# One run of 64x64 matmuls per pair of head pairs: scores of the second token tile in four array quadrants, and a new order of all work

## The chip, the cores and the metric

One Trainium2 chip, of which the program uses one core. The time is that of the device, in microseconds (us), for one execution of the whole program; the time before is 775.9 us, the median of 3 runs (774.52 to 779.68).

## The reference

Attention within chunks of 64 tokens, then a feed-forward part whose nonlinearity is h*cos(h):

```
q, k, v: (8, 8, 576, 64)      # batch, heads, tokens, head dimension
s    = (q_c @ k_c^T) / 8                    # per head and chunk: 64x64
p    = exp(s - max(s)) / (sum + 1e-9)       # over the last axis
x    = p @ v_c, heads side by side          # 4608 tokens x 512
h    = x @ w_in                             # 512 -> 2048
out  = (h * cos(h)) @ w_out                 # 2048 -> 512
```

All is fp32 at the outside. The wide products are made of three fp32r products each (high times high, high times low, low times high).

## The kernel before, in words

The 4608 tokens are 9 tiles of 512. A tile has 8 chunks of 64 tokens and 8 heads, taken as 4 head pairs of 128 partitions (two heads of 64 each). For each tile there are the scores, the softmax, the transposed weights, the weighted values, and from those `x`, which is split in a high and a low part for the feed-forward products.

**Small matmuls.** Scores and weighted values are 64x64 matmuls, which use one quadrant of the 128x128 array each: a quadrant is a half of the rows (where the input partitions stand) and a half of the columns (where the output partitions stand). fp32 matmuls show as two passes each in the profile, so a program's x32 is x64 there. `scores_early` (L525) is for tiles 0 and 1: head 0 of the pair uses the upper left quadrant, head 1 the lower right one, 16 matmuls per head pair into one PSUM bank. `scores_of_pair` (L558) is for tiles 2 to 8: the head chooses the rows, the parity of the chunk the columns, so all four quadrants are used in turn, and two head pairs share two banks (`scores`, L572: 32 matmuls). `weighted_of_pair` (L692) uses four quadrants too.

**Stages.** Tiles 0 and 1 are made plainly: `hidden` (L752, 12 matmuls into a bank `h` for each of 16 blocks of 128 hidden units), `activated` (L764: ScalarE, VectorE, ScalarE, VectorE, then the split of `g`) and `project` (L786). Block s needs the bank of block s-2, which is free when `g<-h,g` (L777) has read it. Tiles 2 to 8 go through a scheme with 7 products for 8 (`two_pairs` L1579, `block_pair` L1848): products A11, S3, S2, A12, S1, A22, S4, in that order, with copies of a bank by ScalarE (L1018) and sums by VectorE (L1021) between them. The attention of a later tile is worked in between these products: `scores_now` (L2285) and `weighted_now` (L2347).

**Order.** The program first writes a list of pieces of work, each with its engine, what it must come after, and an estimated length; then it emits them sorted by the numbers of the table `RANK` (L92), and on the other engine that could do it where the table `ELSEWHERE` (L287) says so (`in_order`, L311). Each engine runs its list strictly as it stands. In `scores_now` and `weighted_now` the 32 matmuls are two pieces of 16, between which the table may put other matmuls; in `early` (L1195), for tile 1, each head pair's scores are a piece.

Of the kernel before, what the change touches and what calls it, by code (L numbers as in the profile page):

```python
# [317 lines left out]
def attention_then_cos_ffn(ctx: ExitStack, tc, qT, kT, v, w_in, w_out, out, wide):  # L318
# [239 lines left out]
    def scores_of_pair(t, g, j, banks):  # L558

        qt, kt = queries.pop((t, 2 * g + j))  # L560
        for c in range(NCH):
# [3 lines left out]
            for h in range(2):  # L565
                hs = slice(h * CH, (h + 1) * CH)
                matmul(
                    banks[h][ps, o : o + CH], qt[hs, cs], kt[hs, cs], start=(o == 0), stop=True,
                    skip_group_check=True,
                )  # L570

    def scores(t, g, banks):  # L572

        for j in range(0 if t > FAST else 2):
            scores_of_pair(t, g, j, banks)
# [2005 lines left out]
```

## Time and profile before

| | |
|---|---|
| median of 3 runs | 775.9 us |
| profiled execution | 775.4 us, span of its records 773.5 us |
| mean granted TensorE clock | 0.998 |
| TensorE (PE) busy | 756.7 us, 98% |
| VectorE (DVE) busy | 675.3 us, 87% |
| ScalarE (ACT) busy | 530.0 us, 69% |
| GpSimd (POOL) busy | 351.8 us, 45% |

PE counts matmuls; a matmul's record runs on after the next has begun, so a distance between two starts tells what one costs, and the duration does not. A row of the timeline merges neighbours of one kind: start, time, what, count, and in brackets the idle time before it with what ended it.

### The profile page before, as it was taken

Reading aid. Unit: us, or ns where it says so; the run is one execution under the profiler, and the core shown is the slowest. Engines: PE = TensorE matmul, PEld = TensorE weight load, DVE = VectorE, ACT = ScalarE, POOL = GpSimd, SP = SyncE. Lnnn points to the kernel's source line nnn. Section 1 sums busy time; section 2 is a strip of 40 time slices with the busy share of each in tenths; the row PEclk is TensorE's granted clock in tenths of the full one; section 3 lists DMA queues with packets and bytes.
Section 4 is the critical chain, followed back from the end, with each engine's and each line's share of the span. In section 5 each row is a group of like instructions: output and inputs, shape, how many; then the busy total and the mean of one; then the engine's idle time right before and its main releaser. Section 6 shows DMA issues by size and latency. Waiting matters only on the chain.

```text
span 773.5 us, 18066 instructions
## 1 busy us (share of the span) xinstructions
PE 756.7 (98%) x6680; PEld 683.9 (88%) x6680; DVE 675.3 (87%) x1129; ACT 530.0 (69%) x1067; POOL 351.8 (45%) x335
## 2 busy tenths in 40 slices
PE   7899999999999999999999999999999999999998
PEld 6688888888999898888889998888899989989997
DVE  4898779889899998989999979989999889878985
ACT  5898787455786466878786659879786556567632
POOL 2443252654589325745732145547501236464143
PEclk9999999999999999999999999999999999999999
DMA  9990631289989857898899956899899567999982
GB/s 345 410 417 28 210 134 57 93 283 342 361 290 332 293 185 247 294 311 258 308 330 380 362 182 240 263 324 326 288 364 342 183 189 251 307 315 337 347 279 99
DMA packets 127001, 210.92 MB, mean 273 GB/s; under 512 B 11713, under 2 KB 67009, under 8 KB 126913
## 3 DMA queue, kind: packets, MB, share of 16 engines
q1 hardware_dynamic: 126336, 208.71, 77.8%
q8 instruction: 53, 0.87, 0.4%
q10 hardware_dynamic: 576, 1.05, 0.4%
q14 instruction: 36, 0.29, 0.1%
HBM read 148.90 MB, written 60.82 MB: 271 GB/s over the span
## 4 chain that ended last, share of the span: by engine, by line
PE 74%; DVE 9%; DMA 8%; ACT 4%; issue 3%; POOL 1%; SPq 0%; ACTq 0%; DVEq 0%; POOLq 0%
PE acc L352 31%; PE h L352 27%; PE a L352 15%; DMA sums<-w_in 4%; DVE w_in L373 2%; DMA w_in<-diffs 2%; DVE w_in L1027 1%; DMA sums<-g 1%; DMA w_in<-in_w_in_dram 1%; DMA x<-sums 1%; ACT w_in L1024 1%; DVE g_lo L373 1%; DVE w_in L686 1%; POOL w_in L373 1%; DVE g L373 1%
## 5 line engine op out<-in xcount | busy, mean ns | idle before, releaser
L352 PE MATMUL h<-x,w_in 128*128 128x512 f32 (+1 forms) x960 | 225.0, 365 | 0.8 <-DVE g L777 0.4
L352 PEld LDWEIGHTS h<-x,w_in 128*128 128x128 f32 x960 | 169.0, 190 | 22.3 <-DVE g L777 1.1
L352 PE MATMUL acc<-w_out,g_hi 128*128 128x512 f32 (+1 forms) x720 | 172.7, 330 | 0.0
L352 PEld LDWEIGHTS acc<-w_out,g_hi 128*128 128x128 f32 x720 | 123.8, 190 | 12.4
L352 PE MATMUL acc<-w_out,g_lo 128*128 128x512 f32 (+1 forms) x360 | 117.4, 326 | 0.0
L352 PE MATMUL h<-w_in,w_in 128*128 128x512 f32 (+1 forms) x384 | 98.7, 355 | 2.0 <-ACT h L1018 1.1
L373 POOL TENSOR_TENSOR w_in<-w_in,w_in 128x512 f32<-128x512 f32 (+2 forms) x41 | 48.8, 1195 | 60.1 <-ACT w_in L1031 27.2
L352 PEld LDWEIGHTS h<-w_in,w_in 128*128 128x128 f32 x384 | 65.4, 190 | 11.8 <-ACT h L1018 3.2
L352 PEld LDWEIGHTS acc<-w_out,g_lo 128*128 128x128 f32 x360 | 68.6, 191 | 4.7
L369 ACT CAST g_hi<-w_in 128x512 fp32r<-128x512 f32 x71 | 44.0, 623 | 34.2 <-PE acc L352 14.9
L1031 ACT ACTIVATE w_in<-w_in 128x512 f32<-128x512 f32 x96 | 57.8, 628 | 12.3 <-DVE w_in L1027 12.0
L373 POOL TENSOR_TENSOR g_lo<-w_in,g_hi 128x512 fp32r<-128x512 f32 x32 | 42.3, 1321 | 38.0 <-ACT g_hi L369 19.2
L373 DVE TENSOR_TENSOR g_lo<-w_in,g_hi 128x512 fp32r<-128x512 f32 x62 | 45.5, 737 | 4.2 <-ACT g_hi L369 3.5
L369 ACT CAST g_hi<-x 128x512 fp32r<-128x512 f32 x52 | 32.2, 622 | 22.4 <-PE acc L352 12.0
L373 POOL TENSOR_TENSOR g_lo<-x,g_hi 128x512 fp32r<-128x512 f32 x9 | 12.3, 1372 | 74.9 <-ACT g_hi L369 74.9
L1024 ACT ACTIVATE w_in<-w_in 128x512 int32<-128x512 f32 x56 | 34.1, 627 | 15.8 <-DVE w_in L1021 11.9
L373 POOL TENSOR_TENSOR g_lo<-g,g_hi 128x512 fp32r<-128x512 f32 x20 | 26.8, 1342 | 38.6 <-ACT g_hi L369 25.7
L352 PE MATMUL a<-w_in,w_in 128*128 128x512 f32 (+1 forms) x204 | 43.1, 350 | 1.0 <-ACT w_in L369 0.7
L352 PE MATMUL a<-x,w_in 128*128 128x512 f32 (+1 forms) x192 | 41.2, 353 | 0.0
L352 PE MATMUL acc<-w_in,g_hi 128*128 128x256 f32 x240 | 41.1, 275 | 0.0
L373 DVE TENSOR_TENSOR g_lo<-x,g_hi 128x512 fp32r<-128x512 f32 x47 | 36.5, 788 | 5.1 <-ACT g_hi L369 4.8
L1027 DVE SCALAR_TENSOR_TENSOR w_in<-w_in,w_in 128x512 f32<-128x512 int32 x56 | 37.7, 696 | 2.4 <-ACT w_in L1024 1.7
(316 smaller groups left out, 1957.4 us busy)
## 6 DMA issues: line engine op xcount, KB each, us to landing
w_in<-combo SPq DMA_DIRECT2D x84, 512.0 KB, 5.4
w_in<-sums SPq DMA_DIRECT2D x64, 256.0 KB, 5.2
combo<-w_in SPq DMA_DIRECT2D x56, 256.0 KB, 4.3
w_in<-combo SPq DMA_DIRECT2D x56, 256.0 KB, 5.5
x<-sums SPq DMA_DIRECT2D x48, 256.0 KB, 5.1
qt<-in_qT_dram SPq DMA_DIRECT2D x36, 256.0 KB, 5.0
w_in<-in_w_in_dram SPq DMA_DIRECT2D x16, 512.0 KB, 9.3
kt<-in_kT_dram SPq DMA_DIRECT2D x32, 256.0 KB, 5.2
```

What stands on the lines that cost most here:

```text
L352: kept(nc.tensor.matmul(*args, **kw))
L369: kept(nc.scalar.copy(out=out, in_=in_))
L373: kept(eng.tensor_tensor(out, a, b, op=op))
L686: kept(nc.vector.transpose(out=dst[o : o + BL, :, qb], in_=src[i : i + BL, :, 1 - qb]))
L1024: kept(nc.scalar.activation(g.bitcast(I32), h, AF.Identity, bias=0.25, scale=0.5 / math.pi))
L1027: kept(nc.vector.scalar_tensor_tensor(g, g.bitcast(I32), -2.0 * math.pi, h, op0=ALU.mult, op1=ALU.add))
L1031: kept(nc.scalar.activation(g, g, AF.Sin, bias=0.5 * math.pi))
```

## The change

1. **Scores of tile 1.** `early(1)` no longer makes them per head pair with two quadrants, but calls `scores` for two head pairs at once, with two banks, as the later tiles do. The quadrant's column half is chosen by `pr % 2` there (every second pair of chunks) and not by the chunk's parity, and the softmax weights stand in another order in their tile (`in_heads`, `at`), since tile 1 is still transposed by TensorE, 128x128 at a time.
2. **Runs undivided.** In `scores_now` and `weighted_now` the two pieces of 16 become one of 32.
3. **New tables.** `RANK` and `ELSEWHERE` are other numbers, for all 3620 pieces. PE has the same instructions as before in kind and number. Of the work that may go to either engine, VectorE has 9 more copies of 128x512 and 11 fewer operations of 128x256, ScalarE 9 fewer of the former, GpSimd 11 more of the latter. ScalarE loads its function table 26 times, before 24.

```
@@ scores_of_pair
             pr, par = divmod(c, 2)
-            cs, ps = slice(c * CH, (c + 1) * CH), slice(par * CH, (par + 1) * CH)
-            o = (j * NPR + pr) * CH
+            row, at = (pr % 2, pr - pr % 2 + par) if t == 1 else (par, pr)
+            cs, ps = slice(c * CH, (c + 1) * CH), slice(row * CH, (row + 1) * CH)
+            o = (j * NPR + at) * CH
...
+    def in_heads(a, t):
+        return a.rearrange("p a (h r) k -> p a r h k" if t == 1 else "p a (r h) k -> p a r h k", h=2)
@@ scores
-        for j in range(0 if t > FAST else 2):
+        for j in range(2):
             scores_of_pair(t, g, j, banks)
-        e = weights_of(t, g).rearrange("p a (r h) k -> p a r h k", h=2)
+        e = in_heads(weights_of(t, g), t)
@@ weighted_of_pair
+                    at = 4 * h + pr if t == 1 else 2 * pr + h
                     matmul(
-                        banks[par][hs, o : o + CH], vt[ks, fs], pts[ks, fs],
+                        banks[par][hs, o : o + CH], vt[ks, fs], pts[ks, at * CH : (at + 1) * CH],
@@ early
-        for hp in range(HP):
-            which = ("a", hp % 2) if t else ("acc", hp)
+        for g in range(2) if t else ():
+            key = ("s", t, g)
+            now = piece(
+                PE, 1.1, made_by(key, lambda g=g: scores(t, g, (bank("a", 0), bank("a", 1)))),
+                banks_free.get(("a", 0)), banks_free.get(("a", 1)), at=max(here["qk", t, 2 * g + j] for j in range(2)),
+                lag=0.35, pairs=64,
+            )
+            below = []
+            for h in range(2):
+                m = piece(DVE, 0.6, rest_of(key, 2 * h), now)
+                below.append(piece(DVE, 0.6, rest_of(key, 2 * h + 1), m, turned_out.get((t - 1, g))))
+                banks_free["a", h] = below[-1]
+            for hp in (2 * g, 2 * g + 1):
+                e[hp] = piece(ACT, 0.6, lambda hp=hp: exponentials_early(t, hp), *below, table=AF.Exp)
+        for hp in () if t else range(HP):
...
@@ scores_now (weighted_now in the same way)
         def go(g=g, t=t):
-            made["banks"] = (h_bank(), h_bank()) if by_h else (bank("a", 1), bank("a", 0))
-            scores_of_pair(t, g, 0, made["banks"])
-
-        def go_on(g=g, t=t):
-            scores_of_pair(t, g, 1, made["banks"])
-            made[g] = scores(t, g, made["banks"])
-
-        pe(0.53, go, *of(names[0]), *of(names[1]), queries_here.get((t, g)))
-        p = pe(0.53, go_on)
+            made[g] = scores(t, g, (h_bank(), h_bank()) if by_h else (bank("a", 1), bank("a", 0)))
+
+        p = pe(1.06, go, *of(names[0]), *of(names[1]), queries_here.get((t, g)))
@@ RANK
-    27, 22, 35, 41, 54, 36, 18, 43, 62, 67, 69, 52, 73, 77, 81, 79, 83, 88, 95, 110, 106, 91, 115, 120, 124, 123,
...
```

In the three places below a name is the tile that an instruction writes, then `<-` and what it reads; the number behind a name tells tiles of one name apart.

**TensorE, scores of tile 1, between the first blocks of `hidden` for tile 0.** Before:

```order
L352 MATMUL h<-x_0_461,w_in_540 128x512
L352 MATMUL a_585<-kt,qt 64x64 x16
L352 MATMUL h<-x_2_523,w_in_491 128x512
...
L352 MATMUL a_618<-kt,qt 64x64 x16
...
L352 MATMUL a_645<-kt,qt 64x64 x16
L656 MATMUL a_675<-ident,e_439 128x128 x4
L656 MATMUL a_686<-ident,e_439 128x128 x4
```

Now, with the first two head pairs before these rows:

```order
L350 MATMUL h_606<-x0_2_508,w_in1_546 128x512
L350 MATMUL a0_627<-kt_239,qt_238 64x64
L350 MATMUL a1_628<-kt_239,qt_238 64x64
...
L350 MATMUL a0_627<-kt_243,qt_242 64x64
L350 MATMUL a1_628<-kt_243,qt_242 64x64
L350 MATMUL h_606<-x0_2_508,w_in1_546 128x512
```

The four runs of 16 have become two of 32 (the first of the four stands ahead of the rows shown). What also moved: the transposes of tile 1's first head pairs (`a<-ident,e`) and the weighted values that use them stood ahead of the third block of `hidden` and stand behind it now.

**TensorE, scores of tile 3, as tile 1 ends.** Before:

```order
L352 MATMUL a_2354<-kt,qt 64x64
L352 MATMUL a_2355<-kt,qt 64x64
L352 MATMUL acc_2294<-w_out_1403,g_hi 128x512 x2
L352 MATMUL acc_2294<-w_out_1403,g_lo 128x512
L352 MATMUL acc_2169<-w_out_1513,g_hi 128x512 x2
L352 MATMUL acc_2169<-w_out_1513,g_lo 128x512
L352 MATMUL a_2354<-kt,qt 64x64
L352 MATMUL a_2355<-kt,qt 64x64
```

Now:

```order
L350 MATMUL a_2467<-kt,qt 64x64
L350 MATMUL a_2468<-kt,qt 64x64
L350 MATMUL h<-kt,qt 64x64 x32
L350 MATMUL acc_2233<-w_out_1607,g_hi 128x512 x2
L350 MATMUL acc_2233<-w_out_1607,g_lo 128x512
```

Before, the first two head pairs are cut in two by six other matmuls, and the other two head pairs come later, in a run of their own. Now all 64 matmuls stand in one run.

**ScalarE, the first table loads after tile 0's softmax.** Before one load, and no other before the third tile's softmax:

```order
L432 ACTIVATE w<-w_out_92 128x512
L621 ACTIVATE e_635<-e_635 128x512
L776 ACT_TABLE_LOAD
L776 ACTIVATE g<-g 128x512
L774 ACTIVATE g<-h 128x512
```

Now three:

```order
L779 ACT_TABLE_LOAD
L779 ACTIVATE g<-g 128x512
L432 ACTIVATE half_90<-w_in_99 128x512
L432 ACTIVATE half_89<-w_out_94 128x512
L777 ACTIVATE g<-h 128x512
L624 ACT_TABLE_LOAD
L624 ACTIVATE e_661<-e_661 128x512 x2
L779 ACT_TABLE_LOAD
L779 ACTIVATE g<-g 128x512
```

The exponentials of tile 1's second two head pairs (`e_661`) have moved behind the first sine (`g<-g`), so the table is changed back and forth once more.

## Rows read from the trace of the kernel before

**Rows 1.** The page, busy time of each engine and share of the span.

```profile
PE 756.7 (98%) x6680; PEld 683.9 (88%) x6680; DVE 675.3 (87%) x1129; ACT 530.0 (69%) x1067; POOL 351.8 (45%) x335
```

**Rows 2.** Stretches of the span: length, then busy time of each engine.

```profile
30.00:36.00 6.00, 4.49 (x109) 3.51 (x108) 5.33 (x11) 4.92 (x8) 3.28 (x3) 1.00 1.02 419
...
40.00:50.00 10.00, 10.00 (x50) 8.77 (x49) 9.65 (x17) 9.74 (x17) 7.04 (x5) 1.00 1.02 418
...
350.00:400.00 50.00, 48.39 (x502) 42.38 (x500) 46.06 (x79) 40.99 (x94) 29.48 (x30) 1.00 0.86 287
```

**Rows 3.** Waits of PE after 36 us: waited for, us, times, longest.

```profile
PE a L352 <- ACT w_in L369: 1.9, 2, 1.2
PE h L352 <- ACT h L1018: 1.1, 4, 0.3
PE h L352 <- DVE w_in L1021: 0.9, 1, 0.9
```

**Rows 4.** Timeline of PE, a whole run of scores: start, us, what, count.

```profile
104.28 0.59 PE L352 MATMUL acc<-w_out,g_hi 128*128 128x512 f32 x2
104.71 0.38 PE L352 MATMUL acc<-w_out,g_lo 128*128 128x512 f32 x1
105.02 1.16 PE L352 MATMUL a<-kt,qt 64*64 64x64 f32 x64
106.11 0.70 PE L352 MATMUL acc<-w_out,g_hi 128*128 128x512 f32 x2
106.65 0.38 PE L352 MATMUL acc<-w_out,g_lo 128*128 128x512 f32 x1
```

**Rows 5.** Timeline of PE, the first half of a divided run.

```profile
185.69 0.69 PE L352 MATMUL a<-kt,qt 64*64 64x64 f32 x32
186.32 0.70 PE L352 MATMUL acc<-w_out,g_hi 128*128 128x512 f32 x2
186.85 0.38 PE L352 MATMUL acc<-w_out,g_lo 128*128 128x512 f32 x1
```

**Rows 6.** Timeline of PE, two runs back to back.

```profile
216.14 1.16 PE L352 MATMUL a<-kt,qt 64*64 64x64 f32 x64
...
218.24 0.70 PE L352 MATMUL acc<-w_out,g_hi 128*128 128x512 f32 x2
218.78 0.38 PE L352 MATMUL acc<-w_out,g_lo 128*128 128x512 f32 x1
```

**Rows 7.** Timeline of PE, scores of tile 1 and the third block.

```profile
25.90 2.21 PE L352 MATMUL h<-x,w_in 128*128 128x512 f32 x9
28.04 1.15 PE L352 MATMUL a<-kt,qt 64*64 64x64 f32 x32
29.12 0.92 PE L352 MATMUL h<-x,w_in 128*128 128x512 f32 x3
...
35.97 1.35 PE L352 MATMUL h<-x,w_in 128*128 128x512 f32 x5 [0.39 <-DVE g L777]
```

**Rows 8.** Timeline of PE, scores followed at once by weighted values.

```profile
15.82 1.56 PE L352 MATMUL a<-kt,qt 64*64 64x64 f32 x29
17.08 0.37 PE L352 MATMUL acc<-pts,vt 64*64 64x64 f32 x2
17.09 0.42 PE L352 MATMUL a<-kt,qt 64*64 64x64 f32 x3
```

**Rows 9.** Timeline of DVE around the start of the third block of `hidden`.

```profile
31.16 0.69 DVE L539 TENSOR_REDUCE m<-a 128x8 f32<-128x512 f32 x1 [0.32 <-PE a L352]
...
33.09 1.28 DVE L367 COPY pts<-a 128x512 f32<-128x512 f32 x2
...
35.22 0.69 DVE L777 TENSOR_TENSOR g<-h,g 128x512 f32<-128x512 f32 x1 [0.25 <-ACT g L776]
35.95 0.43 DVE L367 CAST g_hi<-g 128x512 fp32r<-128x512 f32 x1
```

**Rows 10.** Timeline of ACT, the table load there.

```profile
33.26 1.28 ACT L776 ACT_TABLE_LOAD   x1
```

More of the change, by code (lines that the diff above doesn't have):

```diff
@@ L584, in scores @@
             else:
-                m = sums_of(t)[:, 2 * g : 2 * g + 2].rearrange("p a (r h) -> p a r h", h=2)[:, :, :, h]
+                m = in_heads(sums_of(t)[:, 2 * g : 2 * g + 2].unsqueeze(3), t)[:, :, :, h, 0]
             def largest(m=m, sv=sv):
@@ L713, in weighted @@
         for j, hp in enumerate(hps):
-            if t <= FAST or j:
-                weighted_of_pair(t, hp, j * NPR * CH, banks)
+            weighted_of_pair(t, hp, j * NPR * CH, banks)
         if t >= FAST:
@@ L1197, in early @@
         more_values = None
-        for hp in range(HP):
-            which = ("a", hp % 2) if t else ("acc", hp)
+        for g in range(2) if t else ():
[13 more added lines that the diff above has]
+        for hp in () if t else range(HP):
+            which = "acc", hp
             key = ("s", t, hp)
@@ L1205, in early @@
             m = piece(DVE, 0.6, rest_of(key, 0), s[hp])
-            room = turned_out.get((t - 1, hp // 2))
-            if t == 0 and hp in BY_CHUNK:
+            if hp in BY_CHUNK:
                 m = piece(DVE, 0.25, rest_of(key, 2), m, port=True)
@@ L1210, in early @@
                 continue
-            banks_free[which] = piece(DVE, 0.6, rest_of(key, 1), m, room)
+            banks_free[which] = piece(DVE, 0.6, rest_of(key, 1), m)
             e[hp] = piece(ACT, 0.6, lambda hp=hp: exponentials_early(t, hp), banks_free[which], table=AF.Exp)
@@ L2351, in go @@
         def go(t=t, g=g):
-            made["banks"] = h_bank(), bank("a", 1 - g)
-            weighted_of_pair(t, 2 * g, 0, made["banks"])
-        def go_on(t=t, g=g):
-            made[g] = weighted(t, (2 * g, 2 * g + 1), made["banks"])
-        pe(0.53, go, *(i for n in names for i in of(n)), turned_all[t][g], values_here.get((t, g)))
-        p = pe(0.53, go_on)
+            made[g] = weighted(t, (2 * g, 2 * g + 1), (h_bank(), bank("a", 1 - g)))
+        p = pe(1.06, go, *(i for n in names for i in of(n)), turned_all[t][g], values_here.get((t, g)))
         weighed[t] = [*weighed.get(t, ()), p]
```

421 rows, old and new, of tables (ELSEWHERE, RANK) are left out of this document.

## Prediction

> **What bounds the kernel now.** I read the page's busy times first, then the stretches, then the waits of TensorE, and last the timeline around the 64x64 matmuls. PE is busy 756.7 us, 98% of the span [rows 1]; the next engine, DVE, is at 87%. In the stretches the reader is to see where PE is not alone: between 30 and 36 us it is busy 4.49 of 6 us, while DVE has 5.33 and ACT 4.92; between 40 and 50 us all three are full, DVE 9.65 and ACT 9.74 of 10; between 350 and 400 us PE misses 1.6 us of 50 and DVE works 46.06 [rows 2]. So the program is bound by PE's own work nearly everywhere behind 36 us, and ahead of that by the chain of DVE and ACT that makes the first blocks ready. Behind 36 us the waits come to 5.8 us, all in eight rows, of which the three largest are 1.9 us for a cast of ACT, 1.1 us for ACT's copies of a bank, and 0.9 us for one sum by DVE [rows 3]. A gain on PE behind 36 us therefore reaches the end almost whole; one ahead of it need not.
>
> **What a run of 64x64 matmuls costs.** A plain matmul takes 0.215 us from start to start (two in 0.43 us, 104.28 to 104.71) [rows 4]. From 104.71 to 106.65 us there are three of these and a whole run of 64 passes: 1.94 - 0.65 = 1.29 us; the first pass starts 0.09 us after the matmul ahead of it is due to end. Half a run, from 185.69 to 186.85 us less two matmuls, is 0.73, with the 0.09 ahead 0.82 us [rows 5]. So 32 passes more cost 0.47 us, 15 ns each, and every run pays some 0.35 us at its edges, however short it is: two halves cost 1.64 us, 0.35 us more than a whole one. Two whole runs back to back take 2.64 us to 218.78, less two matmuls, with the 0.09, 2.30 us [rows 6]: 0.28 less than twice 1.29.
>
> **The change, part by part.**
>
> *Runs undivided, and fewer of them.* By the order, PE has 43 runs of 64x64 matmuls before and 32 now. Behind tile 1's first weighted values there are 34 before: 12 halves, 21 whole, one double; and 25 now: 21 whole and 4 doubles. Six pairs of halves made whole give 6 x 0.35 = 2.1 us, three more doubles 3 x 0.28 = 0.8 us. All of it lies behind 36 us, on the engine that sets the end: **-2.9 us**. What a run holds up behind it grows by one half, 0.6 us; PE is in no hurry there, and the engines it feeds have queued work at 46 of 50 us [rows 2].
>
> *Scores of tile 1.* Between the starts at 25.90 and 29.12 us lie nine matmuls and one run of 16 (32 passes): 3.22 - 1.94 = 1.28 us [rows 7]. Less the edges, 0.93 us for 32 passes, 29 ns each: only two quadrants take turns, and each pass is twice as far from the next. Four such runs cost 5.1 us; two runs over four quadrants, at the whole run's price, 2.6. PE is freed of 2.5 us at best. If two quadrants still take turns (below), the 64 passes keep their 30 ns: 2 x 2.25 = 4.5 us, and 0.6 us is freed.
>
> How much of that comes through is set by DVE. The third block of `hidden` starts at 35.97 us, when DVE's product for the first block has let its bank go; that ran at 35.22 [rows 7, 9]. By the order, ahead of this product DVE now has 11 maxima and subtractions of scores where it had 15, at about 0.65 us each (0.69 with the overlap of records), -2.6; one copy of 0.6 fewer; two casts of 0.4 and one quotient, like a subtraction, more [rows 9]: 2.6 + 0.6 - 0.8 - 0.65, so -1.7 us. On the other hand two groups of transposes and one run of weighted values, which I put at 0.43 + 0.43 (four matmuls of 128 columns each, at half the 0.215) and 1.29 us, have moved from before that block to behind it, and PE is full there: +2.15. If DVE idles ahead of the block as much as before, the start is worth +0.45 us, a small loss. If the waits of the chain (PE 1.5 us idle of 6, DVE 0.7, ACT 1.1 [rows 2]) shrink with the shorter runs, it is worth at most what PE is freed of, -2.5. The waits for scores that DVE shows there, such as 0.32 us [rows 9], do go with runs of two head pairs, and DVE's product waited for a sine that had a table load of 1.28 us ahead of it [rows 10], which comes earlier now. I take the middle, **-1.0 us**.
>
> *Two more table loads.* 2 x 1.28 us on ACT [rows 10], both ahead of the second block's sine. That block's bank is asked for by the fourth block, some 5 us of PE work after the third. I cost them at nothing beside that; if the cover is gone they are the fourth rival.
>
> *The rest of the new order.* All waits behind 36 us are dealt anew, 5.8 us of them [rows 3]. One is to be read off: the 0.9 us for a sum by DVE arises where only product A22, 1.3 us, stands between S1 and S4. That is so in 13 of the 24 pairs of the wide scheme before and in 3 now. Against it, only S3 stands between A11 and S2, where ACT's copies are waited for, in 15 pairs, before 11. The work that moved between DVE, ACT and POOL is a few us of hundreds. The casts that are waited for (1.9 us) have the same 5.9 us of PE work between the transfer's release and its use at the one place I counted, so they stay. I take **-0.5 us**, with 3 us to either side.
>
> *Sum.* The profiled execution took 775.4 us, 0.5 below the median of the runs. 775.4 - 2.9 - 1.0 - 0.5 = **771.0 us**.
>
> **The rivals.**
>
> *Two quadrants still take turns.* The scores of tile 1 go in the order upper left, lower left, upper left, lower left (rows by head), then the same on the right. If a matmul may not start before an earlier one, the second pair waits for its quadrants, and the passes stay at 30 ns. Against it: at 17.08 us two passes of the weighted values start while three passes of the scores that stand ahead of them have not [rows 8]; idle quadrants are served out of turn, at least a few matmuls ahead, and four are needed here. Time: 1.9 us less freed, of which DVE's bound hides some: 772.4. The Trainium skill, "TensorE: Matmul & The Clock Gate", Part 3, states the rule: matmuls keep program order in start and in end, and only weight loads overlap. By that rule this rival would hold; the trace's starts disagree. Chance 0.10.
>
> *The waits go.* An order that covers S4 everywhere, and runs that hold no surprise for the engines behind, may remove half of the 5.8 us instead of 0.5: 775.4 - 2.9 - 1.5 - 3.0 = 768.0. For it: 13 thin places become 3. Against it: the longest waits, for casts, keep their cover. Chance 0.16.
>
> *DVE takes the gain.* It empties the banks: a run of 1.1 us asks for four passes of 0.69 us [rows 9], and it works 46.06 of 50 us between 350 and 400 [rows 2]. If PE ahead of time only waits longer for it, the start gives +0.5 and half of the 2.9 us is lost: 775.4 - 1.4 + 0.5 = 774.5. Against it: DVE's share over the span is 87%, and most releases follow PE and move with it. The Trainium skill, "TensorEngine Tiling (Array Packing)", "PSUM Bottleneck", warns of just this: a faster array does not empty PSUM faster. By that rule the scores give nothing and the sum is 772.5; no wait of PE for a maximum or a subtraction behind 36 us bears it out here [rows 3]. Chance 0.10.
>
> *Slower: ACT cannot take the loads.* It works 9.74 of 10 us between 40 and 50 us [rows 2]. If nothing gives, two loads put every block of that stretch 2.6 us later, and the 2.15 us of PE work that moved behind the third block find no room made for them: 775.4 - 2.9 + 2.6 + 2.1 = 777.2. It decides as soon as PE is idle for more than 2 us in all between 36 and 60 us, where it had no idle time at all in the ten us shown. Against it: casts and copies have moved from ACT to DVE in the same stretch. Chance 0.07.
>
> **How the numbers follow.** The forecast has the remaining 0.57; its own range is 771 with 3 us for the waits and 1.5 for the start, taken together as the root of squares some 3.4: 767.5 to 774.5. About 1% of the median, 7.8 us, is what a measurement can tell from no change: faster means below 768.1, slower above 783.7. A seventh of the forecast, 0.08, and half of the case in which the waits go, 0.08, are faster: 0.16. Slower by that much is reached only by something that none of the cases holds: 0.02. The rest, 0.82, is within 1%. The range takes in the middle of the 768.0 case, the 774.5 of DVE and the upper tails: 766.0 to 776.0.
>
> **What would show it right or wrong.** The runs of tile 1's scores should take about 1.1 us for 64 passes in the new timeline; 1.9 us would be the two quadrants. No run of 32 passes should be left behind 60 us, and a run of 64 should still cost 1.29. The third block of `hidden` should start between 32 and 35 us, and PE have under 1 us of idle time from there to 60 us. The waits of PE behind 36 us should sum to between 3 and 8 us, without the 0.9 us for S4; if they sum to 10, the new order and not the runs has decided the time. What would make it all wrong is a wait of several us in one of the later stages, from an order that answers to estimates rather than to this trace.

## The result, and the profile after

| | median | ratio to before, 95% |
|---|---|---|
| kernel before (8 runs) | 776.65 us (774.52 to 779.68) | |
| changed kernel (8 runs) | 782.65 us (780.65 to 784.79) | 1.0075 [1.0054, 1.0096] |

By the ratio the change costs 5.8 us, where 4.9 us of gain were forecast; it is within 1%, but outside the range. The profiled execution took 781.75 us, with a span of 779.7.

The page's busy times, which answer to [rows 1]:

```profile
PE 756.8 (97%) x6680; PEld 683.3 (88%) x6680; DVE 687.3 (88%) x1133; ACT 528.8 (68%) x1060; POOL 360.4 (46%) x340
```

PE is as busy as before. DVE works 12 us longer with four instructions more, GpSimd 8.6 us longer.

The stretches of [rows 2] in the changed kernel (the column before the last two is the granted clock):

```profile
30.00:36.00 6.00, 3.87 (x56) 3.02 (x45) 5.96 (x13) 5.70 (x8) 3.13 (x3) 0.87 1.03 416
40.00:50.00 10.00, 10.00 (x110) 8.62 (x108) 9.97 (x19) 8.53 (x14) 4.00 (x3) 1.00 1.03 418
350.00:400.00 50.00, 48.08 (x436) 42.29 (x435) 48.58 (x84) 40.35 (x93) 26.63 (x27) 1.00 0.89 306
```

Between 350 and 400 us DVE works 48.6 of 50 us, where it had 46.1. The waits of PE behind 36 us, beside [rows 3] (the first five of ten):

```profile
PE h L350 <- ACT h L1021: 3.4, 6, 1.1
PE a L350 <- ACT w_in L367: 2.2, 4, 0.7
PE h L350 <- DVE w_in L1024: 1.6, 2, 1.3
PE a L350 <- ACT e L367: 0.7, 2, 0.5
PE a L350 <- ACT g_hi L367: 0.6, 1, 0.6
```

All ten sum to 9.7 us, where there were 5.8. The forecast had named 10 us as the sign that the new order has decided the time. ACT's copies of a bank went from 1.1 to 3.4 us, and the wait for S4 that the new order was read to remove is 1.3 us long at one place.

The timeline of PE at the start, beside [rows 7]:

```profile
29.45 1.21 PE L350 MATMUL a<-kt,qt 64*64 64x64 f32 x64
30.59 0.92 PE L350 MATMUL h<-x,w_in 128*128 128x512 f32 x3
33.63 4.54 PE L350 MATMUL h<-x,w_in 128*128 128x512 f32 x12 [2.13 <-DVE g L780]
38.01 0.60 PE L659 MATMUL a<-ident,e 128*128 128x128 f32 x4
```

64 passes of tile 1's scores take 1.14 us to the next start: four quadrants work at once. The third block starts at 33.63 us, 2.3 earlier than before, but its 12 matmuls take 4.4 us. This stretch shows why:

```profile
34.40:37.80 3.40, 3.40 (x10) 2.68 (x9) 2.50 (x5) 2.78 (x5) 2.62 (x3) 0.50 1.02 412
```

The granted clock is 0.50, the lower of the two levels, behind 2.1 us in which PE waited. The lower clock does not make the loss, though: the mean granted clock of an execution is 0.991 to 0.998 in the changed kernel, and its two executions at 0.998 took 780.7 and 781.1 us (784.8 at 0.991), where the kernel before takes 774.5 to 775.6 at 0.998 (medians of four sets of runs).

### The profile page after: what moved, and what is told of

The parts are those of the page before. It is cut to its first block, busy times and chain, and to the rows that moved or that the text cites. A ratio compares the mean times of both kernels' runs of the same rounds, so it can differ in the third digit from the quotient of the medians.

```text
span 779.7 us, 18046 instructions
## 1 busy us (share of the span) xinstructions
PE 756.8 (97%) x6680; PEld 683.3 (88%) x6680; DVE 687.3 (88%) x1133; ACT 528.8 (68%) x1060; POOL 360.4 (46%) x340
## 5 line engine op out<-in xcount | busy, mean ns | idle before, releaser
L350 PE MATMUL h<-x,w_in 128*128 128x512 f32 (+1 forms) x960 | 229.2, 369 | 4.0 <-DVE g L780 2.1
L371 POOL TENSOR_TENSOR w_in<-w_in,w_in 128x512 f32<-128x512 f32 (+2 forms) x38 | 44.9, 1188 | 53.3 <-ACT w_in L1034 37.8
L371 DVE TENSOR_TENSOR g_lo<-w_in,g_hi 128x512 fp32r<-128x512 f32 x66 | 50.8, 774 | 6.1 <-ACT g_hi L367 5.2
L371 POOL TENSOR_TENSOR g_lo<-w_in,g_hi 128x512 fp32r<-128x512 f32 x28 | 38.2, 1366 | 34.0 <-ACT g_hi L367 21.1
L1030 DVE SCALAR_TENSOR_TENSOR w_in<-w_in,w_in 128x512 f32<-128x512 int32 x56 | 40.3, 744 | 3.2 <-ACT w_in L1027 2.1
L1027 ACT ACTIVATE w_in<-w_in 128x512 int32<-128x512 f32 x56 | 33.7, 625 | 13.8 <-DVE w_in L1024 10.4
L371 POOL TENSOR_TENSOR g_lo<-g,g_hi 128x512 fp32r<-128x512 f32 x14 | 20.8, 1484 | 45.6 <-ACT g_hi L367 40.7
L350 PEld LDWEIGHTS a<-w_in,w_in 128*128 128x128 f32 x204 | 33.9, 190 | 7.2 <-ACT w_in L367 1.6
L350 PE MATMUL acc<-x,g_hi 128*128 128x256 f32 x232 | 39.7, 275 | 0.0
```

The source lines that it names most:

```text
L350: kept(nc.tensor.matmul(*args, **kw))
L371: kept(eng.tensor_tensor(out, a, b, op=op))
L1027: kept(nc.scalar.activation(g.bitcast(I32), h, AF.Identity, bias=0.25, scale=0.5 / math.pi))
L1030: kept(nc.vector.scalar_tensor_tensor(g, g.bitcast(I32), -2.0 * math.pi, h, op0=ALU.mult, op1=ALU.add))
```

## The experiments

Each result is a median in us and its ratio to the kernel before on the same chip, with the 95% interval. Differences are those of the ratios, turned into us at 776; a difference of two experiments has some 2 us of uncertainty. (The expectation of 14 subtracts medians and so has 7.4 us where the ratios give 5.9.) Two theories at first: the loss sits in the **start** (its timeline shows more idle time and half clock), or in the **rest** of the new order. A cross of the two orders tells them apart. Up to tile 1's weighted values the two orders hold the same steps, the first 277 of before and 275 of the change, so each part can be taken from either table.

**1. Whole runs under the old order.**

```diff
@@ scores_now, weighted_now of the kernel before
-        def go_on: the second half, 16 positions, at its own place
+        both halves in go; go_on issues nothing
```

> The kernel before, its order table untouched, with one edit: the second half of each 64x64 run of the wide scheme is issued where the first half stood (six pairs of halves that had other work between them become whole). Theory 1, the undivided runs are worth what I predicted and harm nothing: 6 x 0.35 = 2.1 us less than before, so about 774.5 where before is 776.6. Rival, undivided runs bring waits of their own (nothing is left between the halves to cover copies and casts): no gain or slower, 776.5 to 779.

775.24 us, ratio 0.9992 [0.9974, 1.0010]: -0.6 us, between the two theories. PE paid less for edges (a whole run takes 1.09 us to the next start where a half took 0.63), but the waits took most of it back: behind 60 us they sum to 6.9 us, before to 5.4, and one product's wait for a cast grew from 0.4 to 1.5 us. This is the row of this kernel:

```profile
PE a L352 <- ACT g_hi L369: 1.5, 1, 1.5
```

The runs are not the loss; their gain of 2.1 us did not come through either (the interval reaches to 2.0).

**2. Old start, new rest.**

```diff
 RANK, ELSEWHERE of the kernel before, runs whole
-steps 277 and on: places and engines of before
+steps 277 and on: places and engines of the change
```

> The first 277 steps of the order (until tile 1's weighted values, some 45 us) as before, with the scores of tile 1 by single head pairs; everything behind them in the new order, runs undivided. Theory 1, the loss of the change sits in the start (its timeline has 5.7 us more of idle time and half clock up to 60 us): this kernel then gains 2 to 3 us on before, 773.5 to 774.5. Theory 2, the new order of the rest costs about as much as the start (waits of PE behind 36 us are 9.7 us against 5.8): gains of the runs and losses of the waits cancel, 776 to 778. If theory 2 alone held, the whole 6 us would be here: 782.

780.86 us, 1.0068 [1.0052, 1.0085]: 5.9 us slower than experiment 1, from the rest alone, and 0.5 from the change. Theory 1 falls.

**3. New start, old rest.**

```diff
 RANK, ELSEWHERE of the change
-steps 275 and on: places and engines of the change
+steps 275 and on: places and engines of before
```

> The other half of the cross: the first 275 steps (four-quadrant scores of tile 1 and what was reordered around them) as in the change, everything behind them in the old order, runs undivided. Theory 1 (the loss is the start): 779 to 781, that is e1 plus 4 to 6 us. Theory 2 (start and rest share it): e1 plus 3 to 4, 777 to 778.5. If the start were worth the 1 us that I forecast, e1 less 1: 773.5.

773.49 us, 0.9972 [0.9956, 0.9987]: 1.6 us faster than experiment 1 and 8.0 faster than the change, with the same four-quadrant scores and whole runs. That agrees with the 1.0 us that was forecast for the start, but 1.6 us is within the uncertainty, and under the new rest the start gives nothing (the change is 0.5 us above experiment 2). PE's waits behind 60 us sum to 5.6 us here and to 9.7 in the change: 4.1 of the 8.0 us. The rest shows as busy time of PE (the stretches under experiments 12 and 13), and no run tells what it is. The timeline has the same start, but a shorter wait and no slow block:

```profile
33.47 2.86 PE L353 MATMUL h<-x,w_in 128*128 128x512 f32 x12 [1.46 <-DVE g L783]
36.17 0.60 PE L662 MATMUL a<-ident,e 128*128 128x128 f32 x4
```

Its granted clock is 1.00 from 34.4 to 37.8 us. Eleven profiled executions have this start with its wait unfilled: the change and experiments 3, 5, 6, 7 and 9 to 14. In eight PE waits 1.46 us there and keeps the clock. In three it waits 2.13 us: the change, and experiments 5 and 6, here in this order:

```profile
32.29 4.51 PE L353 MATMUL h<-x,w_in 128*128 128x512 f32 x12 [2.13 <-DVE g L783]
```

```profile
32.41 2.86 PE L354 MATMUL h<-x,w_in 128*128 128x512 f32 x12 [2.13 <-DVE g L784]
```

So two of the eleven have the slow block, and experiment 6 has the long wait without it. The 1.7 us that the block costs (4.38 us in place of 2.70) come in some executions of this start and not in others; why, is open.

**4. The idle time filled.**

```diff
@@ third block of hidden, changed kernel
+                    for _ in range(18):
+                        kept(nc.tensor.transpose(out=o[:, :P], in_=ident, identity=ident))
```

> The changed kernel with 18 idle transposes of the identity (into a bank of the sums that nobody uses then) in the 2.1 us in which PE waits for the product that lets the third block begin, 31.5 to 33.6 us. They add no data and delay nothing that I can see. Clock theory: the stretch at half clock from 34.4 to 37.8 us goes, the third block of 12 matmuls takes 2.6 us instead of 4.4, and the time falls by up to 1.8 us, to 781. Rival, what follows the third block waits for DVE and ACT anyhow: the third block is quicker but the second tile's last weighted values start at the same time, and the time stays within 0.5 us of the change.

780.38 us, 1.0065 [1.0043, 1.0087], 0.8 us below the change, which does not tell it from nothing. Its profile has a granted clock of 1.00 from 34.4 to 37.8 us; but as most executions of this start keep the clock there without the transposes, this is no test of the clock theory.

**5 and 6. Order and engines crossed.** Within the rest, is it the places or the engines?

```diff
 changed kernel, steps 275 and on
-ELSEWHERE of the change
+ELSEWHERE of before (5); RANK of before with ELSEWHERE of the change (6)
```

> The changed kernel with its new order everywhere, but behind the first 275 steps each copy, cast and subtraction is done by the engine that did it before (324 of the steps behind them have another engine in the change: 162 that it had moved go back, 157 to 167 go back the other way). Theory A, the choice of engines is what costs: DVE works 10 us longer behind 60 us in the new rest (628 to 639 us) with three instructions fewer, because more of them run beside GpSimd. Then this kernel falls most of the way to the 773.5 of the old rest: 774 to 777. Theory B, the order itself costs (the runs of scores stand closer ahead of the products that wait for ACT's copies): it stays at 780 to 783.

> The other half: new start, the old order behind it (as in the kernel that took 773.5), but the engines of the change. Theory A (engines): 779 to 782. Theory B (order): 773 to 775. If the two only fit each other, both mixtures are slower than either whole, since each table of engines was found for its own order: then this one is above 776 and the new order with old engines above 782.

820.02 us (1.0567 [1.0545, 1.0588]) and 812.31 us (1.0467 [1.0444, 1.0490]): 38 us above the change and 38 above experiment 3. Neither theory A nor B: each order fits only the engines that were chosen with it. The last sentence of the expectation of 6 holds.

**7. Three long waits covered.**

```diff
 RANK of the changed kernel, PE
+two products of project ahead of the one that waits at 208.8 us
+four of 0.34 us ahead of the one at 308.9, three ahead of 369.4
```

> The changed kernel with nine products of the second layer moved ahead of three of the products that PE waits longest for: two of 0.65 us each ahead of the one at 208.8 us (wait 0.74), four of 0.34 ahead of 308.9 (1.13), three of 0.34 ahead of 369.4 (1.30). If PE sets the pace and a wait is simply time lost, about 0.7 + 1.1 + 1.0 = 2.8 us go and the kernel takes about 779.8. Rival: the late engines (ACT, DVE) set the pace over longer stretches, so the waits come back at the next products: within 1 us of the change.

782.55 us, 1.0078 [1.0062, 1.0094]: no gain. The waits that were covered did shrink (for ACT's copies of h from 3.4 to 1.2 us, for DVE's sums from 1.6 to 0.6), but all waits behind 60 us sum to 12.0 us, in the change to 9.7. Among them are these, which the change does not have or has at 0.3 us:

```profile
PE acc L354 <- POOL g_lo L375: 1.7, 2, 0.9
PE h L354 <- DMA w_in<-combo: 1.5, 1, 1.5
```

Products that were brought forward now wait themselves, for GpSimd's subtractions (0.9 us at 307.9). At these places there was no ready work to cover with; so the engines behind PE are late, and not PE's order alone is at fault.

**8. The best parts together**: experiment 3 with the transposes of experiment 4, no other edit.

> The kernel with the new start and the old rest, plus the 18 idle transposes in front of the third block. The profile of that kernel without them had no stretch at half clock there (33.5 to 36.2 us at full clock) where the changed kernel's had one, with the same order of the start: so it comes in some executions only. If it comes in about half of them and costs 1.8 us when it does, the median falls by up to 1 us, to 772.5 to 773.5, and the slowest executions go. Rival: the transposes delay the third block or do nothing: 773.5 or up to 0.5 above.

771.93 us (771.41 to 772.74), 0.9943 [0.9928, 0.9957]: faster than before by 4.4 us and than the change by 10. It is 2.2 us below experiment 3, more than expected. The mean granted clock of the executions tells where that comes from: five of these six have 0.998, and two of the twelve of experiment 3, which took 771.8 and 772.0 us, as these do; its other ten have 0.993 to 0.996. The transposes are not shown to be the cause of the better clock: the half-clock stretch of experiment 3's profile lies at 14 to 21 us, ahead of them.

**9 and 10. DVE relieved**, in the change and in experiment 3. Half of the range reduction is left out.

```diff
@@ turn
+        g, h = g[:, :HALF], h[:, :HALF]
         kept(nc.vector.scalar_tensor_tensor(
```

> The changed kernel with the range reduction before the sine (the 96 fused multiply-adds of DVE of 0.68 to 0.74 us each) done on the first half of the columns only; the other half keeps its integers, which the sine then takes as they are. It takes some 96 x 0.3 = 29 us from DVE and leaves every instruction in its place. Theory A2, DVE is what comes late in the new rest: the time falls by 5 us or more, to 775 to 777.5. Theory B2, the order of ACT's and GpSimd's queues makes the waits: it falls by less than 2 us, 781 or more.

> The same relief of DVE in the kernel with the new start and the old rest (773.5 without). Its PE waits for DVE for less than 1 us behind 60 us, so I expect 1 to 2 us less, about 772. By theory A2 the two relieved kernels lie within 4 us of each other (9 without relief); by theory B2 7 us or more apart.

775.29 us (0.9999 [0.9980, 1.0018]) and 771.83 us (0.9950 [0.9932, 0.9968]): the change gains 5.9 us by this, the old rest 1.7. They end 3.8 us apart, as theory A2 has it, if narrowly. The new rest has less room for DVE's work than the old one; whether DVE's surplus made the loss, this does not tell, since the relief (some 24 us of DVE) is twice the surplus.

**11. ACT relieved**, changed kernel; one maximum serves four chunks.

```diff
@@ raised
-                for r in range(NPR): exponentials of 64 columns with their own maximum
+                one exponential of 256 columns; its sum copied to the other three
```

> The changed kernel in which ACT takes the exponentials of four chunks by one instruction of 256 columns (with the first chunk's maximum and one sum for all four, copied to the other three), not by four of 64: some 0.5 us less for each of 24 such groups, 12 us of ACT, just ahead of the copies that PE waits for (3.4 us of waits for ACT's copies of h). If ACT's queue at these places sets the time: 2 to 3 us less, 779.5 to 780.5. If DVE does: within 1 us of the change, 781.7 or more.

779.17 us, 1.0036 [1.0015, 1.0056]: 3.0 us less. The wait for ACT's copies falls from 3.4 to 1.3 us:

```profile
PE h L350 <- ACT h L1021: 1.3, 3, 0.6
```

So ACT's queue has its share. Whether that is separate from DVE's is not shown: ACT's exponentials wait for DVE's maxima in both orders, as the timeline below shows.

**12. More work for GpSimd**, on experiment 3.

```diff
@@ the loop that issues the steps
+            if n_pool % 16 == 0:
+                for _ in range(4):
+                    kept(nc.gpsimd.tensor_tensor(ident, ident, ident, op=ALU.mult))
```

> The kernel with the new start and the old rest, plus 64 products of the identity with itself on GpSimd (128x128, four after every sixteenth of its subtractions), whose result nobody reads: some 25 us more work for GpSimd (the new rest has 15 more). DVE's instructions between SBUF tiles take 687 ns alone and 800 to 1,100 beside GpSimd; those that read PSUM take 681 to 687 either way. Theory A3, this crowding is how the new rest makes DVE late: DVE's time behind 60 us goes from 629 to 640 us or more and the kernel takes 777 to 781. Rival: DVE gets busier but had room, and the time stays under 775.

783.76 us, 1.0112 [1.0085, 1.0139]: 10.9 us slower, but not by the path that was expected. Behind 60 us, first experiment 3 and then this (PE, PEld, DVE, ACT, POOL):

```profile
60.00:780.00 720.00, 701.48 (x6045) 637.77 (x6043) 629.02 (x1042) 483.58 (x978) 328.77 (x311) 1.00 0.77 261
```

```profile
60.00:780.00 720.00, 703.30 (x6044) 637.93 (x6042) 631.00 (x1042) 483.21 (x977) 358.39 (x375) 1.00 0.77 261
```

GpSimd has 29.6 us more, DVE 2.0 and not 11. GpSimd's queue being late is enough to delay all, though it was busy for only 45% of the span without the addition. It reaches PE mostly through the other engines: the waits of PE behind 60 us go from 5.6 to 13.8 us, those for GpSimd itself from nothing to 0.3, and the one for DVE's sums from 0.3 us to this:

```profile
PE h L353 <- DVE w_in L1027: 3.7, 4, 1.5
```

Theory A3 is not borne out by it, and a run with the surplus on DVE alone was needed.

**13 and 14. DVE's surplus alone**: given to the good rest, taken from the bad one.

```diff
@@ 13: the loop that issues the steps, experiment 3
+            if n_dve % 16 == 0:
+                kept(nc.vector.tensor_tensor(ident, ident, ident, op=ALU.mult))
@@ 14: turn, changed kernel (a quarter of the range reduction left out)
+        g, h = g[:, : 3 * P], h[:, : 3 * P]
```

> The kernel with the new start and the old rest (773.5), plus 61 products of the identity with itself on DVE (128x128, one after every sixteenth of its instructions behind the start), whose result nobody reads: about 61 x 0.2 = 12 us more work for DVE, the surplus that the change's rest has on it (639 to 641 us behind 60 us where the old rest has 629). If the surplus by itself accounts for the loss, the time rises by 5 to 9 us, to 778.5 to 782.5. If DVE has room for 12 us more (it is idle for 91 of 720 us there) and the order is at fault: 773 to 775.5.

> The changed kernel with the range reduction on three quarters of the columns: DVE is relieved by some 12 us, its surplus, and not by the 23 that the relief to one half took off. If the surplus accounts for the loss, most of the 7.4 us that the larger relief gave are there already: 775 to 777.5. If it is the order that leaves no room and any relief helps by its size: about half of it, 778.5 to 780.

778.85 us (1.0046 [1.0027, 1.0064]) and 778.00 us (1.0036 [1.0018, 1.0055]). Behind 60 us the change, then 13, then 14:

```profile
60.00:780.00 720.00, 705.35 (x6053) 639.95 (x6052) 640.57 (x1041) 483.33 (x974) 342.90 (x320) 1.00 0.77 261
```

```profile
60.00:780.00 720.00, 704.07 (x6042) 637.84 (x6040) 645.60 (x1102) 483.72 (x977) 332.74 (x311) 1.00 0.76 261
```

```profile
60.00:780.00 720.00, 701.59 (x6043) 637.58 (x6041) 626.09 (x1037) 480.53 (x972) 341.87 (x320) 1.00 0.76 260
```

In 13 DVE has 16.6 us more than in experiment 3 and the time is 5.7 us longer: 0.34 us for each. In 14 it has 14.5 less than in the change, and the time is 3.0 shorter: 0.21 for each. Experiment 13 lies in the range that was named for the surplus, but with 16.6 us where 12 were meant; 14 lies between its two ranges, at half of what experiment 9 gained. At these rates the change's surplus of 11.6 us is worth 2.4 to 3.9 of the 8.0 us (an estimate). Experiment 14 says it more directly: there DVE has 626.1 us behind 60 us, less than the 629.0 of the old rest, and the kernel is still 5.0 us slower than experiment 3. So some 4.1 to 5.6 us, each figure uncertain by some 2, belong to the order of the new rest and not to how much DVE has to do.

## How a wait arises in the new rest

One place of many is shown: the scores at some 300 us and product S2 behind them, which waits for ACT's copy. Changed kernel, PE, then ACT, then DVE:

```profile
303.37 1.16 PE L350 MATMUL a<-kt,qt 64*64 64x64 f32 x64
...
310.39 0.48 PE L350 MATMUL h<-w_in,w_in 128*128 128x512 f32 x1 [1.13 <-ACT h L1021]
```

```profile
306.27 1.28 ACT L603 ACT_TABLE_LOAD   x1 [1.17 <-DVE m L598]
...
309.72 0.62 ACT L1021 COPY h<-h 128x512 f32<-128x512 f32 x1
```

```profile
301.49 1.82 DVE L1030 SCALAR_TENSOR_TENSOR w_in<-w_in,w_in 128x512 f32<-128x512 int32 x2
...
305.22 0.68 DVE L591 TENSOR_REDUCE m<-a 128x8 f32<-128x512 f32 x1
```

The same step with the old rest (experiment 3), PE, ACT and DVE:

```profile
297.67 1.16 PE L353 MATMUL a<-kt,qt 64*64 64x64 f32 x64
...
306.37 0.48 PE L353 MATMUL h<-w_in,w_in 128*128 128x512 f32 x1 [0.21 <-ACT h L1024]
```

```profile
302.23 1.28 ACT L606 ACT_TABLE_LOAD   x1 [1.79 <-DVE m L601]
...
305.70 0.61 ACT L1024 COPY h<-h 128x512 f32<-128x512 f32 x1
```

```profile
299.65 0.68 DVE L594 TENSOR_REDUCE m<-a 128x8 f32<-128x512 f32 x1
```

And PE's time on `project` (tile `acc`) from the scores to S2, in the change and then in experiment 3:

```profile
303.37:310.39 7.02, 2.28 (x10) 1.00 0.79 254
```

```profile
297.67:306.37 8.70, 4.96 (x21) 1.00 0.80 287
```

The copy stands in ACT's queue behind the exponentials of these scores in both, and they wait for DVE's maxima. From scores to S2 PE has 7.0 us in the change, 1.1 of them idle, and 8.7 in the old order, 0.2 of them idle. Three groups of `project`, of three matmuls and 0.65 us each, stand between where seven stood (the tenth matmul of the first row is the end of one ahead of the scores); two of the four stand ahead of the scores now. That is 2.6 us less cover. The queues behind are not later here: DVE's first maximum starts 1.9 us behind the scores (2.0 in the old order) and ACT's copy 6.4 us behind them (8.0), though DVE takes 1.82 us just before for two operations that take 0.68 each elsewhere. The cover fell by 2.6 us and the copy came 1.7 us sooner, so the wait grew by 0.9. Cover on PE has a price only against the moment when the copy is ready, and that is set in two other queues.

The surplus of DVE lies in operations between SBUF tiles. Added up by shape, DVE's records behind 60 us come to 12.1 us more in the change than in experiment 3: 1.7 of it because DVE does other operations (nine more copies out of PSUM, 6.2 us, against smaller ones fewer), 10.3 because operations between SBUF tiles take longer (casts of 128x512 563 ns on average and not 466, subtractions to fp32r 792 and not 753), and nothing from those that read PSUM. One operation, experiment 3, then the change (behind 60 us: busy, mean ns, idle before):

```profile
L1033 DVE SCALAR_TENSOR_TENSOR w_in<-w_in,w_in 128x512 f32<-128x512 int32 x56 | 38.0, 701 | 2.5 <-ACT w_in L1030 1.8
...
L1033 DVE SCALAR_TENSOR_TENSOR w_in<-w_in,h 128x512 f32<-128x512 int32 x40 | 27.3, 682 | 9.0 <-ACT w_in L1030 8.7
```

```profile
L1030 DVE SCALAR_TENSOR_TENSOR w_in<-w_in,w_in 128x512 f32<-128x512 int32 x56 | 40.3, 744 | 3.2 <-ACT w_in L1027 2.1
...
L1030 DVE SCALAR_TENSOR_TENSOR w_in<-w_in,h 128x512 f32<-128x512 int32 x40 | 27.2, 681 | 6.6 <-ACT w_in L1027 6.5
```

The same operation with one operand in PSUM keeps its 681 ns. Laid against GpSimd's records, those of the 56 with under a tenth of their time beside GpSimd take 686 ns in the change; the 11 that share a tenth to nine tenths of it take 882 (up to a half) and 1,020 ns (above) on average, though four of them keep 681 to 693. For all sums, products and subtractions of 128x512 between SBUF tiles (TENSOR_TENSOR) it is the same: 686 ns with under a tenth beside GpSimd, about 980 with over half; of the latter the change has 92 and experiment 3 69, where they take about 1,010. Those that read PSUM take 681 to 686 either way. The Trainium skill, "Advanced Engine Details and Errata", "VectorE Performance Modes", says that VectorE's second SBUF port is shared with GpSimd, and that GpSimd's instructions and VectorE's two-port ones block each other. These rows agree so far as VectorE is held up beside GpSimd only in SBUF; which of its operations here are two-port ones no run shows.

## Why the prediction was wrong

- **The rest of the new order, -0.5 us with 3 to either side: this step failed.** It measures +5.9 (old start, against experiment 1) to +8.0 us (new start, against experiment 3), and this includes the three more doubles, forecast at -0.8. I read one pattern off PE's order (what stands between S1 and S4), set it against another, and called the moves between engines a few us of hundreds. In DVE's work they are that: 1.7 us net behind 60 us. (Besides the moves listed under the change, DVE has taken six operations of 128x512 from GpSimd.) But the same operations take 10.3 us longer where the new order lays them beside GpSimd's, and 324 steps had changed engine: experiments 5 and 6 show that order and engines are worth 38 us when they don't fit each other. I counted covers on PE and did not follow the queues of DVE, ACT and GpSimd to the waiting product.
- **Runs undivided, -2.9 us.** The six joined pairs, 2.1 of it, gave 0.6 by themselves (experiment 1): the edges went, and 1.5 us of new waits took their place. "A gain on PE behind 36 us reaches the end almost whole" was the wrong premise, since 5.8 us of waits said only how late the others were, not how little room they had: 16.6 us more for DVE cost 5.7, 29.6 for GpSimd 10.9.
- **Start, -1.0 us.** The mechanism was right: four quadrants work at once, and the third block began within the time named. The size agrees with -1.6 under the old rest, but not with +0.5 under the new one, and with 2 us of uncertainty neither tells it from nothing.
- **Two table loads, at nothing.** Nothing in the cross speaks against it. PE is busy all 22 us from 38 to 60 us, so the slower rival did not come about; its 777.2 was nearest to the result by luck, with another mechanism and in another place.
- **DVE takes the gain** (774.5) named an engine that does hold the new rest up and gave it too little: a loss of half the gain, where DVE's own time grew, by an amount that is worth 2.4 to 3.9 us.
- **Half clock** was in no step. In the profiled execution it cost 1.7 us in the third block; at equal mean clock the loss is the same, so the forecast did not fail by it.

Open: how the 4.1 to 5.6 us that DVE's surplus does not explain are shared by PE's own order and by ACT's and GpSimd's queues. Experiments 11 and 12 show that relief of ACT can give 3.0 us and more work on GpSimd take 10.9, not how much either did here.

## What to carry to other kernels

Where four in-order queues feed each other, price a new order by following the queue behind each wait, or by running it in parts: a cross of old and new order at a point where both have done the same steps found the loss in two runs and a better kernel beside it (773.5 us). A wait of PE is a symptom: here covering three of them gave nothing, and relieving DVE gave 5.9 us. A table of engines belongs to the order it was found with, by 38 us in this kernel; take both or neither.

## What the runs showed of the hardware

- 64x64 matmuls issued in the order A B A B, C D C D over the four quadrants run at 15 to 16 ns a pass, where two quadrants in turn took 30 (the starts of tile 1's scores in the change and before).
- The same order of the start gave PE two clocks for the third block: 0.50 behind a wait of 2.13 us in two executions, 1.00 behind such a wait in a third and behind 1.46 us in eight others.
- An engine at 45% of the span (GpSimd) cost the kernel 0.37 us for each us of work that was added to it.
- DVE's 128x512 operations on two tensors in SBUF take 686 ns alone and about 980 with over half of their time beside GpSimd's; with an operand in PSUM they take 681 to 686 either way.
